# Windowed attention into a gated convolutional expert: stretches of 384 tokens with wide matmuls, gates on two chunks at once, and a different preparation of the first eight head pairs and of the weights

## The chip, the cores and the metric

The kernel runs on one core of a Trainium2 chip. A core has a tensor engine (PE, with a weight-load side PEld), a vector engine (DVE), a scalar engine (ACT), GpSimd (POOL) and SyncE (SP, which here issues the transfers). The metric is the device time of one execution in microseconds, the median of several runs. All times below are microseconds unless marked ns.

## The reference

```python
# q, k, v: (8, 8, 576, 64); batch 8, heads 8, sequence 576, head size 64
scores = q @ k^T / 8
# heads 0-3: 0 <= i - j < 32;  heads 4-7: 0 <= i - j < 128 and (i - j) % 4 == 0
scores = where(mask, scores, -1e9)
attn = exp(scores - max); attn = attn / (sum + 1e-9)
x = (attn @ v) laid out as (8, 576, 512)
h = relu(x @ w_in)                        # 512 -> 1024
conv = conv_w[0]*h[s-1] + conv_w[1]*h[s] + conv_w[2]*h[s+1]    # along the sequence, per channel
out = (h * sigmoid(conv)) @ w_out         # 1024 -> 512
```

Inputs and outputs are float32; the weights `w_in`, `w_out` and `conv_w` arrive as float64.

## The kernel before

**Attention.** It is computed for a batch and a pair of heads at a time (32 pairs: 8 batches times 4). Only 64 keys are scored for each block of 32 queries. On PE, `scores` (L248) issues 76 or 72 small matmuls into an `att` tile of PSUM. DVE then adds the mask (L254, L257), takes the maximum of each of the nine slots of 64 keys (L260) and subtracts it (L262). ACT takes the exponential of the whole 128x576 tile (L264). DVE sums it by slot (L266), adds 1e-9 (L268), inverts (L270), multiplies (L271) and transposes (L273). `values` (L283) issues 96 small matmuls. The result goes from PSUM to two float32r tiles, a high part `x..a` (ACT, L320) and the low rest `x..b`: subtracted by DVE (L335), or for the first two batches (`HELPED`) by PE with a negated identity (`minus`, L327 and L330) and copied by ACT (L333).

**Expert.** `expert(b)` works on a batch of 576 tokens. Every product of float32 operands is three float32r matmuls (high*high, high*low, low*high: `TERMS`). `first` (L353) multiplies by `w_in`: 8 chunks of 128 channels, each in two halves of 288 tokens, so 192 matmuls of 288 columns with the weights stationary. ACT applies relu (L360). The gate of each chunk of 576 tokens is ACT L371 (middle tap), twice DVE L365 (outer taps), ACT L376 (sigmoid), DVE L378 (times h), ACT L380 (high part `g..a`), DVE L382 (low part `g..b`). `second` (L395) multiplies by `w_out` with the weights stationary: 4 chunks of the output, 2 halves, 8 chunks of the sum, 3 terms, again 192 matmuls of 288 columns. ACT copies out of PSUM (L402), SP sends.

**Weights.** A float64 chunk of 128x512 is turned into a float32r high and low part by integer steps: ACT L428, DVE L430, L433, L435, L438, L441. For the first ten of the sixteen chunks (`SUMMED = 10`) PE adds the two words and forms the rest (L450, an fp32 matmul with the identity, L451 and L452 with `minus`; ACT L447 and L455 copy). For the other six DVE does it (L457, L463).

**What sets the order.** The program is written out as tasks with an engine, a cost, a due time, predecessors and buffers. `Planner.order` lists them for all engines once, when the program is built; a task that is ready and due first is taken. The due times are the tables `DUE`, `PAIR`, `WI`, `WO`, from the third batch on with a fixed period. Each engine works through its own list in order. Buffers are counted: two `qk`, three `v`, two `pt`, seven `x`, eight `g`, three `h`, three `c`, two PSUM banks each for `mm` and `nn`, and one `att` of four banks.

## Time and profile before

| | |
|---|---|
| median of 3 runs | 549.85 (548.9 to 550.44) |
| profiled execution, span first to last instruction | 549.1 |
| TensorE clock, mean granted | 0.990 |
| PE / PEld / DVE / ACT busy | 522.4 / 497.2 / 415.7 / 298.1 |
| instructions | 19084 |
| HBM read / written | 41.66 MB / 9.44 MB |

What lies around the span of the profiled execution is not listed for it; its span is 0.75 below the median of the timed runs. "Busy" is the time in which at least one instruction of the engine was under way; PE's matmuls are pipelined, so their own durations overlap (a 288-column matmul has 296 ns, and the next starts long before that). How long a matmul holds the engine is read from the chain of work that ended last, where a run of matmuls is one piece with its count.

### The profile page before, as it was taken

To read this page: it belongs to the slowest core of one execution; us is meant where nothing else is said; L and a number is where in the kernel's file an instruction comes from. 1 tells how busy PE (TensorE), PEld (TensorE's weight loads), DVE (VectorE), ACT (ScalarE), POOL (GpSimd) and SP (SyncE) were. 2 spreads that over 40 slices of the span, in tenths; PEclk is the share of its full clock that TensorE was granted. 3 is DMA by queue.
4 is the path that set the end of the run, shared out by engine and by line. 5 is a ranking of instruction groups with operands and counts; after the bars stand their busy time and mean duration, and the time that the engine had idled before them with its cause. 6 is when DMAs were issued, how large, how long until landed. Compare 5 with 4: busy or idle time off the path is not lost.

```text
span 549.1 us, 19084 instructions
## 1 busy us (share of the span) xinstructions
PE 522.4 (95%) x8664; PEld 497.2 (91%) x8664; DVE 415.7 (76%) x695; ACT 298.1 (54%) x556; POOL 0.9 (0%) x12
## 2 busy tenths in 40 slices
PE   3499978999999999999999999999999999999997
PEld 2468876999999999999999999999989999999997
DVE  4968998899997389946998389946988389946920
ACT  2457784855752486337742486237742486337721
POOL 0000000000000000000000000000000000000000
PEclk9999996999999999999999999999999999999999
DMA  7756513331044102630055102530045102300011
GB/s 247 268 157 215 195 52 137 119 121 44 7 138 152 30 23 65 200 110 23 13 161 170 32 23 72 190 113 23 17 152 162 45 23 58 117 26 23 0 44 44
DMA packets 17072, 52.31 MB, mean 95 GB/s; under 512 B 2016, under 2 KB 3168, under 8 KB 16992
## 3 DMA queue, kind: packets, MB, share of 16 engines
q1 hardware_dynamic: 16848, 51.02, 27.8%
q8 instruction: 68, 1.11, 0.9%
q10 hardware_dynamic: 144, 0.08, 0.1%
q14 instruction: 12, 0.10, 0.1%
HBM read 41.66 MB, written 9.44 MB: 93 GB/s over the span
## 4 chain that ended last, share of the span: by engine, by line
PE 92%; DVE 3%; ACT 2%; DMA 2%; issue 1%; ACTq 0%
PE nn L395 38%; PE mm L353 35%; PE att L283 8%; PE att L248 6%; PE nn L450 2%; PE nn L353 2%; PE att L327 1%; DMA qk<-in_qk_d_dram 1%; DMA qk<-in_qk_p_dram 1%; PE nn L451 0%; PE nn L452 0%; DVE pt L273 0%; DVE s L271 0%; PE att L330 0%; DVE c L365 0%
## 5 line engine op out<-in xcount | busy, mean ns | idle before, releaser
L365 DVE SCALAR_TENSOR_TENSOR c<-h,conv_sb,c 128x576 f32<-128x576 f32 x128 | 103.9, 815 | 48.4 <-ACT c L371 46.9
L360 ACT ACTIVATE h<-mm 128x288 f32<-128x288 f32 x120 | 48.8, 408 | 50.4 <-PE mm L353 50.1
L402 ACT COPY out<-nn 128x288 f32<-128x288 f32 x64 | 25.5, 400 | 70.1 <-PE nn L395 66.1
L378 DVE TENSOR_TENSOR c<-c,h 128x576 f32<-128x576 f32 x64 | 47.6, 755 | 9.4 <-ACT c L376 7.8
L283 PEld LDWEIGHTS att<-pt,v 32*64 32x64 f32 x3072 | 40.8, 138 | 14.8 <-DVE s L257 4.6
L283 PE MATMUL att<-pt,v 32*64 32x64 f32 (+2 forms) x3072 | 44.2, 232 | 9.4 <-DVE s L257 3.5
L371 ACT ACTIVATE c<-h,conv_sb 128x576 f32<-128x576 f32 x64 | 49.7, 776 | 1.3
L248 PE MATMUL att<-qk 64*32 64x64 f32 x2432 | 36.2, 235 | 11.0 <-DMA qk<-in_qk_d_dram 5.5
L248 PEld LDWEIGHTS att<-qk 64*32 64x32 f32 x2432 | 30.2, 111 | 16.9 <-DMA qk<-in_qk_d_dram 5.5
L376 ACT ACTIVATE c<-c 128x576 f32<-128x576 f32 x64 | 42.5, 678 | 2.1 <-DVE c L365 1.6
L353 PE MATMUL mm<-x2a,wi 128*128 128x288 f32 x144 | 40.5, 296 | 0.0
L353 PE MATMUL mm<-x1a,wi 128*128 128x288 f32 x144 | 40.3, 296 | 0.0
L353 PE MATMUL mm<-x3a,wi 128*128 128x288 f32 x144 | 40.3, 295 | 0.0
L353 PE MATMUL mm<-x0a,wi 128*128 128x288 f32 x144 | 40.3, 295 | 0.0
L395 PE MATMUL nn<-g2a,wo 128*128 128x288 f32 x128 | 37.0, 304 | 0.0
L395 PE MATMUL nn<-g0a,wo 128*128 128x288 f32 x128 | 36.4, 299 | 0.2
L395 PE MATMUL nn<-g6a,wo 128*128 128x288 f32 x128 | 36.6, 299 | 0.0
L395 PE MATMUL nn<-g3a,wo 128*128 128x288 f32 x128 | 36.4, 299 | 0.0
L395 PE MATMUL nn<-g1a,wo 128*128 128x288 f32 x128 | 36.4, 299 | 0.0
L395 PE MATMUL nn<-g4a,wo 128*128 128x288 f32 x128 | 36.4, 299 | 0.0
L395 PE MATMUL nn<-g5a,wo 128*128 128x288 f32 x128 | 36.4, 299 | 0.0
L395 PE MATMUL nn<-g7a,wo 128*128 128x288 f32 x128 | 36.1, 300 | 0.1
(194 smaller groups left out, 1502.5 us busy)
## 6 DMA issues: line engine op xcount, KB each, us to landing
...
```

The costliest lines, as they stand in the source:

```text
L248: nc.tensor.matmul(sc.t[quad * 32:quad * 32 + 32, slot // 4, slot % 4 * W:slot % 4 * W + W], q, k, start=i == 0, stop=i == len(parts) - 1, ...
L283: nc.tensor.matmul(tv.t[hd * 64:hd * 64 + 64, bank, o:o + n], v.t[quad * 32:quad * 32 + 32, block // 2, block % 2 * 64:block % 2 * 64 + 64 ...
L327: nc.tensor.matmul(tv.t[:, t, 0:128], minus, main[:, t], start=False, stop=True, skip_group_check=True)
L353: nc.tensor.matmul(ps.t[:, 0:HALF], wi[jw][fc][:, k * 128:k * 128 + 128], x[k].t[jx][:, hf * HALF:hf * HALF + HALF], start=(k == 0 and i = ...
L360: relu.append(plan.add("ACT", 0.4, due + 1.6 * u + 1.6, lambda fc=fc, hf=hf, ps=ps: nc.scalar.activation(out=h[fc].t[:, 1 + hf * HALF:1 + ...
L365: nc.vector.scalar_tensor_tensor(out=c[fc].t, in0=h[fc].t[:, k:S + k], scalar=conv_sb[:, k, fc:fc + 1], in1=c[fc].t, op0=ALU.mult, op1=ALU ...
L371: t = plan.add("ACT", 0.777, d, lambda fc=fc: nc.scalar.activation(out=c[fc].t, in_=h[fc].t[:, 1:S + 1], func=AF.Copy, scale=conv_sb[:, 1, ...
L376: t = plan.add("ACT", 0.686, d + 1.0, lambda fc=fc: nc.scalar.activation(out=c[fc].t, in_=c[fc].t, func=AF.Sigmoid), [t], [c[fc]], "sigmoid")
L378: t = plan.add("DVE", 0.755, d + 1.5, lambda fc=fc: nc.vector.tensor_tensor(out=c[fc].t, in0=c[fc].t, in1=h[fc].t[:, 1:S + 1], op=ALU.mult ...
L395: nc.tensor.matmul(ps.t[:, 0:HALF], wo[jw][2 * dm + k // 4][:, k % 4 * 128:k % 4 * 128 + 128], g[k].t[jg][:, hf * HALF:hf * HALF + HALF], ...
L402: outs.append(plan.add("ACT", 0.4, out_due + 3.3 + 3.3 * u, lambda hf=hf, ps=ps, o=o: nc.scalar.copy(out=o.t[:, hf * HALF:hf * HALF + HALF ...
L450: nc.tensor.matmul(ps.t, ident, t(), start=True, stop=False)
```

## The change

The expert works on stretches of 384 tokens, two segments of 192, three stretches to two batches (`expert(u)`, 12 stretches). `x` of two neighbouring batches lies in one wide tile per pair with a zero column between, and `first` (L410) computes both segments with a token more at each side: 388 columns. `second` (L452) turns the operands round: the gated tokens are stationary (128 of them), `w_out` streams with 512 columns, and the output has tokens on partitions. The gates handle the taps chunk by chunk (384 columns) and the sigmoid and the products two chunks at once (768 columns). There are five `g` tiles of two chunks and two `h` tiles of two chunks.

For the first eight pairs (`SLOTS`, `MASKS`, two batches) PE adds the mask by a bf16 identity before the scores (L269), DVE takes the negated maximum straight from PSUM (L288) and scales it (L295), and ACT takes the exponential in nine instructions, one for each slot, with the maximum as bias and the sum as a second output (L300). All sixteen weight chunks are summed by PE (`SUMMED = 16`). The due times are a new table without a period.

```diff
-HALF = S // 2
+UNITS = 3
+SEG, SEGS = S // 3, 2
+HALO = SEG + 2
+UNIT = SEGS * SEG
+XB = S + 1
+XW = 2 * XB + 2
+SLOTS, MASKS, HELPED = 0xff, 0xff, 0xff
+SUMMED = 16
+DUE = {
...
+    "pair": ((268.04, 269.22, 317.89, -93.12), (361.15, 413.68, 341.56, 430.48), ...
-    slots("x", 7, [128, S], F32R, 2)
-    slots("g", NF, [128, S], F32R, 2)
-    hs = slots("h", 3, [128, S + 2])
-    slots("c", 3, [128, S])
+    xt = [[const.tile([128, XW], F32R, name=f"x{p}{'ab'[j]}") for j in range(2)] for p in range(NP)]
...
+    slots("g", 5, [128, 2, UNIT], F32R, 2)
+    slots("h", 2, [128, 2 * SEGS, HALO])
+    slots("c", 3, [128, 2 * SEGS, SEG])
-    SUMMED = 10
-    HELPED = 2
+        def masks():
+            for i, n in enumerate((256, 256, W)):
+                nc.tensor.matmul(sc.t[:, i, 0:n], eye, mask_sb[:, kind, 256 * i:256 * i + n], start=True, stop=False,
+                                 skip_group_check=True)
+        if masked:
+            lq = plan.add("PE", 0.27, due, masks, [lq], [qk, sc, s], "E")
+            if masked:
+                for i, cost in enumerate((0.68, 0.215)):
+                    last = plan.add("DVE", cost, due + 2.0, lambda i=i: nc.vector.tensor_reduce(
+                        out=(m.t[:, 0:8].rearrange("p (h a) -> p h a", h=2), m.t[:, 8:9])[i],
+                        in_=(sc.t[:, 0:2, 0:256].rearrange("p h (a k) -> p h a k", k=W), sc.t[:, 2, 0:W])[i],
+                        axis=AX.X, op=ALU.max, negate=True), [last], [sc, s, m])
+            last = plan.add("DVE", 0.173, due + 2.5, lambda: nc.vector.tensor_scalar(
+                out=m.t, in0=m.t, scalar1=SCALE, scalar2=None, op0=ALU.mult), [last], [m])
+            def exps():
+                for i in range(9):
+                    nc.scalar.activation(out=s.t[:, i], func=AF.Exp,
+                                         in_=sc.t[:, i // 4, i % 4 * W:i % 4 * W + W] if masked else s.t[:, i], bias=m.t[:, i:i + 1],
+                                         scale=SCALE, accum_out=z.t[:, i:i + 1])
...
+            def first(fc, ps, k):
                 for i, (jw, jx) in enumerate(TERMS):
+                    nc.tensor.matmul(ps.t[:, 0:SEGS * HALO], wi[jw][fc][:, k * 128:k * 128 + 128], window(xt[k][jx]),
+                                     start=(k == 0 and i == 0), stop=(k == NC - 1 and i == 2))
...
+        for i in range(NF // 2):
+            d, convs = gated + 3.94 * i, []
+            for fc in (2 * i, 2 * i + 1):
+                t = plan.add("ACT", 0.617, ... AF.Copy, scale=conv_sb[:, 1, fc:fc + 1]), [relu[fc], conved], [h[i], c[i]])
+                for k in (0, 2):
+                    t = plan.add("DVE", 0.617, d + 0.5 + fc % 2, lambda fc=fc, k=k: tap(fc, k), [t], [h[i], c[i]])
+                convs.append(t)
+            t = plan.add("ACT", 0.846, ... AF.Sigmoid), convs, [c[i]], "sigmoid")
+            t = plan.add("DVE", 0.957, ... op=ALU.mult), [t], [c[i], h[i]])
+            hi = plan.add("ACT", 0.835, ... nc.scalar.copy(out=split(g[i].t[0]), in_=c[i].t), ...
+            gates.append(plan.add("DVE", 0.957, ... op=ALU.subtract), [hi], [c[i], g[i]]))
+        for j in range(UNIT // 128):
+            def second(j, ps, k):
                 for i, (jw, jg) in enumerate(TERMS):
+                    nc.tensor.matmul(ps.t, g[k // 2].t[jg][:, k % 2, j * 128:j * 128 + 128], wo[jw][k],
+                                     start=(k == 0 and i == 0), stop=(k == NF - 1 and i == 2))
+            for k in range(NF):
+                last = plan.add("PE", 0.648, out_due + 5.2 * j + 0.65 * k, lambda a=(j, ps, k): second(*a),
+                                [last, *(wored if u == 0 else []), gates[k // 2]], [ps, g[k // 2]], "E")
```

The order is settled when the program is built, so it can be shown for three places. In the rows a name is followed by its buffer's number; `g0a` and `g0b` are the high and low part of a gate tile, `wi_67` and `wo_84` are weight tiles.

PE, before, behind the first batch's `first` products: two weight chunks and a pair's rest, then the first matmuls of `second`, then the next pair's `values`.

```order
L450 MATMUL nn_163<-w0b,ident 128x512
L451 MATMUL nn_163<-r_157,minus 128x512
L452 MATMUL nn_163<-wo_82,minus 128x512
L327 MATMUL att_159<-x6a,minus 128x128 x4
L330 MATMUL att_159<-x6a,minus 128x32 x2
L450 MATMUL nn_162<-w1b,ident 128x512
L451 MATMUL nn_162<-r_158,minus 128x512
L452 MATMUL nn_162<-wo_83,minus 128x512
L395 MATMUL nn_163<-g0a,wo_82 128x288
L395 MATMUL nn_163<-g0b,wo_82 128x288
L395 MATMUL nn_163<-g0a,wo_90 128x288
L283 MATMUL att_159<-pt_113,v_101 64x64 x24
```

PE, after, at the corresponding place. The first `second` matmuls of the first stretch (L452) stand behind `first` matmuls (L410) of the second stretch.

```order
L410 MATMUL mm_148<-x3a,wi_68 128x388
L410 MATMUL mm_148<-x3b,wi_68 128x388
L410 MATMUL mm_148<-x3a,wi_76 128x388
L264 MATMUL att_147<-qk_100 32x64 x36
L452 MATMUL nn_151<-wo_83,g0a 128x512
L452 MATMUL nn_151<-wo_83,g0b 128x512
L452 MATMUL nn_151<-wo_91,g0a 128x512
L410 MATMUL mm_149<-x0a,wi_69 128x388
L410 MATMUL mm_149<-x0b,wi_69 128x388
L410 MATMUL mm_149<-x0a,wi_77 128x388
L410 MATMUL mm_149<-x1a,wi_69 128x388
L410 MATMUL mm_149<-x1b,wi_69 128x388
```

The ten PE-summed chunks stood ahead of the first `second` matmul, and now all sixteen do; between the first three matmuls of `second` and its next 21 PE now has four runs of twelve `first` matmuls and a pair's scores.

DVE, before, at the first gates of the first batch: a tile is one chunk of 576 tokens.

```order
L378 TENSOR_TENSOR c_147<-c_147,h_144 128x576
L378 TENSOR_TENSOR c_148<-c_148,h_145 128x576
L365 SCALAR_TENSOR_TENSOR c_149<-h_146,conv_sb,c_149 128x576
L382 TENSOR_TENSOR g0b<-c_147,g0a 128x576
L254 TENSOR_TENSOR s_103<-att_159,mask_sb 128x512
L382 TENSOR_TENSOR g1b<-c_148,g1a 128x576
L257 TENSOR_TENSOR s_103<-att_159,mask_sb 128x64
L378 TENSOR_TENSOR c_149<-c_149,h_146 128x576
L260 TENSOR_REDUCE m_106<-s_103 128x9
L262 TENSOR_TENSOR s_103<-s_103,m_106 128x576
L382 TENSOR_TENSOR g2b<-c_149,g2a 128x576
```

One instruction made one gate tile's step, and the maximum of a pair (L260) stood between. DVE, after, at the gates of the first stretch (`g0b` to `g3b` are what the 21 matmuls behind the rows above read): a tile is two chunks of 384.

```order
L439 TENSOR_TENSOR c_135<-c_135,h_133 128x768
L439 TENSOR_TENSOR c_136<-c_136,h_134 128x768
L443 TENSOR_TENSOR g0b<-c_135,g0a 128x768
L443 TENSOR_TENSOR g1b<-c_136,g1a 128x768
L306 TENSOR_REDUCE m_109<-s_106 128x9
L423 SCALAR_TENSOR_TENSOR c_137<-h_133,conv_sb,c_137 128x384 x2
L308 TENSOR_TENSOR s_106<-s_106,m_109 128x576
L423 SCALAR_TENSOR_TENSOR c_137<-h_133,conv_sb,c_137 128x384 x2
L423 SCALAR_TENSOR_TENSOR c_135<-h_134,conv_sb,c_135 128x384 x2
L439 TENSOR_TENSOR c_137<-c_137,h_133 128x768
L423 SCALAR_TENSOR_TENSOR c_135<-h_134,conv_sb,c_135 128x384 x2
L282 TENSOR_TENSOR s_104<-att_147,mask_sb 128x512
```

Each product and split now covers two chunks, and steps of a later batch's attention (L282, L306, L308) stand between the gates of the first stretch.

PE at the end of the program, before: the last `first` matmuls of the last batch, then the `second` matmuls of the same batch alone.

```order
L353 MATMUL mm_161<-x3a,wi_73 128x288
L353 MATMUL mm_161<-x3b,wi_73 128x288
L353 MATMUL mm_161<-x3a,wi_81 128x288
L353 MATMUL mm_161<-x0a,wi_73 128x288
L353 MATMUL mm_161<-x0b,wi_73 128x288
L353 MATMUL mm_161<-x0a,wi_81 128x288
L395 MATMUL nn_163<-g0a,wo_82 128x288
L395 MATMUL nn_163<-g0b,wo_82 128x288
L395 MATMUL nn_163<-g0a,wo_90 128x288
```

PE at the end of the program, after: the last `first` matmuls of the last stretch (into `mm_148`), then `second` of the stretch ahead of it (reading `g0`), whose 48 matmuls stand before the last stretch's 72.

```order
L410 MATMUL mm_148<-x2a,wi_74 128x388
L410 MATMUL mm_148<-x2b,wi_74 128x388
L410 MATMUL mm_148<-x2a,wi_82 128x388
L410 MATMUL mm_148<-x3a,wi_74 128x388
L410 MATMUL mm_148<-x3b,wi_74 128x388
L410 MATMUL mm_148<-x3a,wi_82 128x388
L452 MATMUL nn_151<-wo_83,g0a 128x512
L452 MATMUL nn_151<-wo_83,g0b 128x512
L452 MATMUL nn_151<-wo_91,g0a 128x512
L452 MATMUL nn_151<-wo_84,g0a 128x512
L452 MATMUL nn_151<-wo_84,g0b 128x512
L452 MATMUL nn_151<-wo_92,g0a 128x512
```

The last batch's own products stood directly behind its gates; now another stretch's products lie between.

More of the change, by code (lines that the diff above doesn't have):

```diff
@@ L167, in attn_moe @@
     minus = const.tile([128, 128], F32R, name="minus")
+    eye = const.tile([128, 128], BF16, name="eye")
     wi = [[const.tile([128, 512], F32R, name=f"wi{j}{c}") for c in range(NF)] for j in range(2)]
-    wo = [[const.tile([128, 512], F32R, name=f"wo{j}{c}") for c in range(2 * NC)] for j in range(2)]
+    wo = [[const.tile([128, DM], F32R, name=f"wo{j}{c}") for c in range(NF)] for j in range(2)]
     plan = Planner()
@@ L260, in attention @@
-        last = plan.add("DVE", 0.755, due + 2.0, lambda: nc.vector.tensor_reduce(
-            out=m.t, in_=s.t, axis=AX.X, op=ALU.max), [last], [s, m])
-        last = plan.add("DVE", 0.755, due + 2.5, lambda: nc.vector.tensor_tensor(
-            out=s.t, in0=s.t, in1=wide(m.t), op=ALU.subtract), [last], [s, m])
-        last = plan.add("ACT", 0.685, due + 3.0, lambda: nc.scalar.activation(
-            out=s.t, in_=s.t, func=AF.Exp, scale=SCALE), [last], [s], "exp")
-        last = plan.add("DVE", 0.755, due + 3.5, lambda: nc.vector.tensor_reduce(
-            out=z.t, in_=s.t, axis=AX.X, op=ALU.add), [last], [s, z])
+        two = lambda t: (halves(t[:, 0:512]), t[:, 512:576])
@@ L332, in attention @@
             last = plan.add("PE", (0.42, 0.6)[kind], due + 7.2, less, his, [tv, x], "E")
             return [plan.add("ACT", cost, due + 7.5, lambda i=i: nc.scalar.copy(out=parts(x.t[1])[i], in_=src(i)),
-                             [last], [tv, x]) for i, cost in ((0, (0.62, 1.12)[kind]), (1, (0.25, 0.3)[kind]))]
-        return [plan.add("DVE", cost, due + 7.5, lambda i=i: nc.vector.tensor_tensor(
+                             [last], [tv, x]) for i, cost in pieces]
+        return [plan.add("DVE", cost + 0.06 * (1 - i), due + 7.5, lambda i=i: nc.vector.tensor_tensor(
@@ L346, in expert @@
         relu = []
-        for u in range(2 * NF):
-            fc, hf = u // 2, u % 2
-            ps, last = Buffer("nn" if b == 0 and u % 4 > 1 else "mm"), None
-            def first(fc, hf, ps, k):
+        for fc in range(NF):
+            ps, last = Buffer("nn" if u == 0 and fc % 2 else "mm"), None
+            def first(fc, ps, k):
                 for i, (jw, jx) in enumerate(TERMS):
-                    nc.tensor.matmul(ps.t[:, 0:HALF], wi[jw][fc][:, k * 128:k * 128 + 128],
-                                     x[k].t[jx][:, hf * HALF:hf * HALF + HALF],
+                    nc.tensor.matmul(ps.t[:, 0:SEGS * HALO], wi[jw][fc][:, k * 128:k * 128 + 128], window(xt[k][jx]),
@@ L355, in first @@
                                      start=(k == 0 and i == 0), stop=(k == NC - 1 and i == 2))
             for k in range(NC):
-                last = plan.add("PE", 0.396, due + 1.6 * u + 0.4 * k, lambda a=(fc, hf, ps, k): first(*a),
-                                [last, wired[fc], *(ready[k] if b == 0 else sum(ready, []))], [ps, x[k]], "E")
-            relu.append(plan.add("ACT", 0.4, due + 1.6 * u + 1.6, lambda fc=fc, hf=hf, ps=ps: nc.scalar.activation(
-                out=h[fc].t[:, 1 + hf * HALF:1 + hf * HALF + HALF], in_=ps.t[:, 0:HALF], func=AF.Relu),
-                [last], [ps, h[fc]]))
+                last = plan.add("PE", 0.493, first_due + 1.97 * fc + 0.49 * k, lambda a=(fc, ps, k): first(*a),
+                                [last, wired[fc], *(t for b in used for t in (ready[b][k] if u == 0 else sum(ready[b], [])))],
+                                [ps, *x[k]], "E")
@@ L364, in tap @@
+            relu.append(plan.add("ACT", 0.49, first_due + 1.97 * fc + 1.97, lambda fc=fc, ps=ps: nc.scalar.activation(
+                out=both(h[fc // 2].t, fc).rearrange("p a k -> p (a k)"), in_=ps.t[:, 0:SEGS * HALO], func=AF.Relu),
+                [last], [ps, h[fc // 2]]))
         def tap(fc, k):
-            nc.vector.scalar_tensor_tensor(out=c[fc].t, in0=h[fc].t[:, k:S + k], scalar=conv_sb[:, k, fc:fc + 1],
-                                           in1=c[fc].t, op0=ALU.mult, op1=ALU.add)
+            t = both(c[fc // 2].t, fc)
@@ L368, in expert @@
+            nc.vector.scalar_tensor_tensor(out=t, in0=both(h[fc // 2].t, fc)[:, :, k:k + SEG], in1=t,
+                                           scalar=conv_sb[:, k, fc:fc + 1], op0=ALU.mult, op1=ALU.add)
+        split = lambda t: t.rearrange("p f (a k) -> p (f a) k", a=SEGS)
         gates = []
[L369 to L384 removed]
```

177 lines of the change are left out of this document (96 added, 81 removed).

## The prediction

> **What bounds the kernel now.** I read the page's busy times first, then the chain that ended last, then that chain in order of time, then a table by stretches, and last the groups by line.
>
> ```profile
> span 549.1 us, 19084 instructions
> PE 522.4 (95%) x8664; PEld 497.2 (91%) x8664; DVE 415.7 (76%) x695; ACT 298.1 (54%) x556; POOL 0.9 (0%) x12
> ...
> PE 92%; DVE 3%; ACT 2%; DMA 2%; issue 1%; ACTq 0%
> ```
>
> The first line is the span. The second gives busy time, share and instructions of each engine. The last gives the shares of the chain that ended last: PE carries 92% of it. The span of this execution stands 0.75 below the median of 549.85; the sum is made against 549.1, and 0.75 is added at the end.
>
> ```profile
> 0.00:94.60 94.60, 72.76 (x1556) 61.03 (x1557) 80.54 (x157) 54.47 (x103) 0.90 (x12) 0.95 0.53 184
> ...
> 140.00:518.70 378.70, 378.00 (x6429) 365.89 (x6428) 289.45 (x464) 207.34 (x387) 0.00 (x0) 1.00 0.24 79
> 518.70:526.20 7.50, 6.94 (x48) 6.19 (x46) 5.48 (x8) 4.20 (x8) 0.00 (x0) 1.00 0.01 2
> ```
>
> Each row is a stretch, its length, then busy time (and instructions) of PE, PEld, DVE, ACT, POOL, then clock and transfers. From 140 to 518.7 PE is busy 378.0 of 378.7, DVE 289.5 (76%), ACT 55%. So the middle is PE's alone. In the first 94.6, when the first `second` matmul starts, PE is busy 72.8, while DVE is busy 80.5 (85%): the head waits on DVE.
>
> ```profile
> 305.80 7.94 PE mm L353 x60
> 316.54 16.30 PE mm L353 x123
> 367.45 7.94 PE mm L353 x60
> ```
>
> A row of this chain is a start, how long that piece held the path, and its instructions. The same piece of 60 matmuls starts at 305.80 and at 367.45: a batch takes 61.65. One matmul of 288 columns holds PE 16.30/123 = 0.1325, so its 384 take 50.9, and the other 10.8 are four pairs' scores and values, 2.69 each with the changes between matmul shapes.
>
> ```profile
> 53.08 0.86 PE nn L450 x2
> 53.94 0.23 PE nn L451
> 54.18 0.23 PE nn L452
> ...
> 58.18 0.39 PE att L327 x4
> 58.57 0.18 PE att L330 x2
> ...
> 81.98 1.27 PE att L283 x76
> ...
> 90.35 0.43 PE nn L451
> 90.78 0.43 PE nn L452
> ```
>
> In the head, a weight chunk takes 0.86 + 0.23 + 0.23 = 1.32 and a pair's rest by PE 0.39 + 0.18 = 0.57. PE's own work is therefore 8 × 61.65 + 10 × 1.32 + 8 × 0.57 = 511.0, and 38.1 of the span is something else. PE's last run ends at 545.6 (the tail rows below), which leaves 3.5 behind it; in 518.7 to 526.2, where the last gates are finished, PE does 48 matmuls (6.4) in 7.5, a loss of 1.1; 33.5 are left for the head. There, between 74.26 and 81.98, the path leaves PE altogether, and afterwards the same L451 and L452 take 0.43 instead of 0.23, at the clock of 0.50 of this row:
>
> ```profile
> 84.00:93.00 9.00, 8.18 (x113) 6.42 (x114) 8.79 (x17) 4.09 (x8) 0.00 (x0) 0.50 0.54 183
> ```
>
> ```profile
> 526.24 19.36 PE nn L395 x144
> 545.66 0.40 ACT out L402
> ```
>
> **The wide matmuls.** `first` has 12 × 8 × 4 × 3 = 1152 matmuls of 388 columns for 1536 of 288; `second` has 12 × 3 × 8 × 3 = 864 of 512 for 1536. Columns are 889,344 against 884,736, so all that can be gained is what a matmul costs beside its columns. No 388 is in the trace, but 512 is: L452 (128x512, float32r, another weight load behind it) holds the path 0.23. From 288 to 512 that is 0.0975 for 224 columns, so 388 takes 0.176. Sum: 1152 × 0.176 + 864 × 0.230 = 401.5 against 3072 × 0.1325 = 407.0: 5.5 less. Lower bound: at the clock of 0.50 L451 and L452 take 0.43; if all of that scaled with the clock, 512 would take 0.215 and 388 0.163, together 373.6, 33.4 less than now. Upper bound: if cost follows columns at the 288 rate, 0.1785 and 0.2356, together 409.2, 2.2 more. I take 0.230, since it is measured at full clock in the same form. The weight load does not explain the 288 row: the L327 row loads four full weights in 0.39, 0.1 each.
>
> The Trainium skill (TensorE: Matmul & The Clock Gate, section "Wait — 56ns, not 53.3ns?") gives a warm matmul as columns/2.4 plus about 2.5 ns. By it 512 would take 0.2158, 388 0.1642 and 288 0.1225; this trace has 0.23 and 0.1325, so it disagrees on both that can be compared.
>
> **More for PE.** Six more chunks summed by PE: 6 × 1.32 = 7.9, on the path. Masks: three bf16 matmuls for each of eight pairs, 576 columns; between nothing and the 0.39 of L327's four, near the latter: 0.3 × 8 = 2.4. The rest by PE stays 8 × 0.57. PE's work becomes 511.0 − 5.5 + 7.9 + 2.4 = 515.8.
>
> **DVE.**
>
> ```profile
> L365 DVE SCALAR_TENSOR_TENSOR c<-h,conv_sb,c 128x576 f32<-128x576 f32 x128 | 103.9, 815 | 48.4 <-ACT c L371 46.9
> L378 DVE TENSOR_TENSOR c<-c,h 128x576 f32<-128x576 f32 x64 | 47.6, 755 | 9.4 <-ACT c L376 7.8
> L254 DVE TENSOR_TENSOR s<-att,mask_sb 128x512 f32<-128x512 f32 x32 | 21.8, 680 | 2.4 <-PE att L248 2.3
> L257 DVE TENSOR_TENSOR s<-att,mask_sb 128x64 f32<-128x64 f32 x32 | 6.6, 208 | 0.0
> L262 DVE TENSOR_TENSOR s<-s,m 128x576 f32<-128x576 f32 x32 | 24.1, 753 | 0.7
> L266 DVE TENSOR_REDUCE z<-s 128x9 f32<-128x576 f32 x32 | 23.7, 739 | 0.4 <-ACT s L264 0.3
> L268 DVE TENSOR_SCALAR z<-z 128x9 f32<-128x9 f32 x32 | 5.4, 170 | 0.9
> L270 DVE RECIPROCAL z<-z 128x9 f32<-128x9 f32 x32 | 6.9, 215 | 1.0
> L271 DVE TENSOR_TENSOR s<-s,z 128x576 f32<-128x576 f32 x32 | 24.2, 758 | 1.0
> L273 DVE STREAM_TRANSPOSE pt<-s 128x576 f32<-128x576 f32 x32 | 24.8, 776 | 0.9
> L435 DVE SCALAR_TENSOR_TENSOR w1b<-out,w1b 128x512 int32<-128x512 int32 x8 | 5.5, 686 | 0.1
> L438 DVE TENSOR_SCALAR w0a<-w0b 128x512 int32<-128x512 int32 x8 | 3.4, 422 | 0.1
> L463 DVE TENSOR_TENSOR wo<-w1b,wo 128x512 fp32r<-128x512 f32 x3 | 2.1, 688 | 0.0
> ```
>
> Behind the first bar stand busy us and mean ns. 512 against 64 elements (L254, L257) is 1.05 ns an element, so a tap of 384 takes 0.815 − 0.20 = 0.613, a step of 768 0.755 + 0.20 = 0.957. Gates of all batches: 192 × 0.613 + 96 × 0.957 = 209.6 against 128 × (0.815 + 0.755) = 201.0: +8.6, hidden in the middle, where DVE has 24% free; if that cover goes, see the rivals. In each of the eight first pairs the mask adds (0.888), the subtraction (0.753) and the sum (0.739) go, the scale (0.170) comes, and the maximum is read from PSUM in two pieces (0.888 for about 0.74): 2.06 less, 16.5 in all. Six chunks lose two steps of 0.688: 8.3 less. Both fall in the head.
>
> **The head.** The 21 `second` matmuls of the first stretch wait for `g3b`. Ahead of it the new order has on DVE: 16 chunks of 3 × 0.422 + 2 × 0.686 = 2.64 (42.2); eight pairs of 0.680 + 0.208 + 2 × 0.170 + 0.215 + 0.758 + 0.776 = 2.98 (23.8); four steps each of two later pairs (4.8); 16 taps (9.8); eight steps of 768 (7.7); about 3 for masks and conv weights: 91.3. Neighbours overlap a little: means times counts over all DVE rows make 442 where the page has 415.7 busy, so 91.3 is 85.8 busy. At the 85% of the head before, `g3b` is done at 101. PE's work ahead of that place is 168 × 0.176 + 3 × 0.230 + 16 × 1.32 + 8 × 0.57 + 8 × 0.3 + 11 scores and 8 values (9.5 × 2.69) = 83.8. Transfers are not in the way: the same 16 chunks and eight pairs come on SP, in another order, and the output is the same bytes in 36 transfers for 36. GpSimd zeroes more columns beside the first transfer.
>
> ```profile
> L264 ACT ACTIVATE s<-s 128x576 f32<-128x576 f32 x32 | 21.3, 684 | 21.8 <-DVE s L262 21.7
> L455 ACT CAST wi<-nn 128x512 fp32r<-128x512 f32 x8 | 4.7, 584 | 6.1 <-PE nn L452 6.0
> L333 ACT CAST x1b<-att 128x64 fp32r<-128x64 f32 x2 | 0.6, 284 | 0.0
> L360 ACT ACTIVATE h<-mm 128x288 f32<-128x288 f32 x120 | 48.8, 408 | 50.4 <-PE mm L353 50.1
> ```
>
> ACT has 54.5 busy in the first 94.6. Nine exponentials of 64 replace one of 576: from 512 to 64 elements (L455, L333) is 0.3 less, so 0.684 shrinks to about 0.3 each, the second output unseen. It could be free (0.27) or double it (0.6); I take 0.3, since L333's 0.284 is the nearest row. That is 8 × (2.7 − 0.684) = 16.1, and six more copies of 0.584, 3.5: 74 of 101, under DVE's 86. In the middle ACT is 45% free, and its instructions there get fewer and wider (relu 96 × 0.49 for 128 × 0.408). Behind the nine stand on ACT the copies of weight chunks (L499, L507), for which PE's sums wait.
>
> There is one `att` tile, and scores and values of all pairs take turns in it. Before, the scores left it with the mask add; now the nine exponentials read it.
>
> ```profile
> 0.74 4.69 DMA qk<-in_qk_d_dram
> ...
> 342.39 1.06 PE att L248 x66
> 363.18 1.29 PE att L283 x81
> ```
>
> A pair holds it for 0.3 + 1.06 + 0.888 + 0.170 + 2.7 = 5.1 from the mask to the last exponential, and for 1.29 + 0.87 + 0.57 + 0.87 = 3.6 from the values to the last copy: 8.7. Eight pairs make 69.6, three later pairs' scores and mask adds 5.8, and the first transfer lands at 5.4: 81 with no wait between the steps. Each pair changes engine eight times, and behind engines this busy each change may wait half of an instruction of 0.6: 8 × 8 × 0.3 = 19, together 100. Two bounds, 101 and 100, that hinder each other: I take 103. The head then loses 103 − 83.8 = 19 where it lost 33.5. What is late next is this tile, ahead of DVE: scores that wait for it hold every matmul behind them on PE.
>
> **The end.** The last gates now run beside the preceding stretch's 48 matmuls, 48 × 0.23 = 11.0, longer than a chain of about 0.49 + 0.62 + 2 × 0.61 + 0.84 + 0.96 + 0.83 + 0.96 = 5.9 (ACT steps by 0.8 ns an element from their rows); the 1.1 goes. The last copy is 0.584 for 0.40 and its transfer nearly doubles: 3.5 becomes 4.0.
>
> Sum: 515.8 + 19 + 4.0 = 538.8, plus 0.75: 539.6, so 540.
>
> **Rivals.** *Wide matmuls shed their fixed cost* (lower bound, 0.163 and 0.215): 27.9 less, 512. For it: the low-clock rows show no fixed part. Against: L452 shows 0.23 every time at full clock. The Trainium skill's formula, above, would come out beside it (1.4 and 0.7 more in sum, about 514); the trace has so far not followed it. *Cost follows columns*: 7.7 more, 547. For it: 0.1325/288 and 0.23/512 differ by 2.4%. *The `att` tile bounds the head*, the case on the other side: if an exponential with its sum takes 0.6 instead of 0.3, every pair holds the tile 2.7 longer, 8 × 2.7 = 21.6, the 21 matmuls start at about 122 and the head loses 38: 515.8 + 38 + 4.75 = 559. It decides from a head of 115 (a loss of 31), that is from about 0.47 an exponential. For it: no row shows an exponential of 64 or a second output. Against it: a copy of 64 from PSUM takes 0.284 (L333). *The middle waits on the gates*: five `g` tiles of two chunks and two `h` tiles let gates lead by little; DVE's 50 of 60 us a batch would have to leave PE idle 3% to give back all: 550. Against it: DVE then still has a sixth free. *No gain in the head*, where the change does not do what it says there, gives 515.8 + 33.5 + 4.75 = 554.
>
> **Chances.** Forecast (532 to 546) 0.50; shed cost (506 to 524) 0.24; by columns (546 to 549) 0.05; waits in the middle (547 to 556) 0.08; the `att` tile or no gain in the head (548 to 562) 0.13. The range leaves out the ends of the outer cases, about 0.2 in all: 509 to 552. The three runs of before lie within 0.3%, about what tells a change from none. Faster by more than that (under 548.2): 0.50 + 0.24 + 0.04 + 0.03 = 0.81; within it (to 551.5): 0.06; slower: 0.13.
>
> **What would show it.** Chain pieces of `first` at 0.176 a matmul and `second` at 0.230 (0.163 and 0.215 for the first rival, 0.236 for the second); the first 21-matmul run of `second` at about 103; L300 at about 300 ns; PE over 98% busy from 120 to the end; nothing but a copy and a transfer behind the last matmul. The prediction is wrong if the head is late because the exponentials hold `att`, if PE's rows wait for `g` in the middle, or if the wide rows are far from 0.176 and 0.230.

## The result, and the profile after

The changed kernel takes 557.59 (median of 4 runs, 556.71 to 558.69) against 549.92 of the kernel before on the same chip: ratio 1.0137, interval 1.0112 to 1.0162. It is slower; the forecast was 540.

The page of its profiled execution (556.71; span, busy times, the chain's shares):

```profile
span 554.9 us, 17158 instructions
PE 528.1 (95%) x7656; PEld 456.8 (82%) x7656; DVE 401.7 (72%) x700; ACT 328.1 (59%) x652; POOL 1.5 (0%) x30
...
PE 92%; ACT 5%; DVE 1%; DMA 1%; issue 0%; ACTq 0%; DVEq 0%
```

The chain in order of time, after: the last runs ahead of the 21 `second` matmuls of the first stretch (24 with the three behind them), long runs of `second` and `first` in the middle, and the end.

```profile
109.66 8.56 PE mm L410 x48
118.22 0.90 PE att L264 x58
119.12 5.67 PE nn L452 x24
...
149.66 16.37 PE nn L452 x72
...
225.60 17.08 PE mm L410 x96
...
524.02 27.24 PE nn L452 x120
```

A matmul of 388 columns holds PE 17.08/96 = 0.178, one of 512 16.37/72 = 0.227; behind the last one 3.6 are left. The 21 matmuls start at 119.12, and not because they wait for the gates: DVE's step for `g3b` (L443) starts at 113.76 and takes 0.95, so it is done at 114.7, while PE still has 4.4 of earlier work to do. Stretches, after (columns as in the prediction):

```profile
0.00:62.00 62.00, 39.69 (x847) 27.08 (x847) 42.31 (x97) 35.45 (x135) 1.50 (x30) 0.81 0.65 221
0.00:94.60 94.60, 72.29 (x1486) 54.09 (x1487) 68.26 (x151) 61.02 (x221) 1.50 (x30) 0.87 0.59 200
140.00:518.70 378.70, 378.67 (x5264) 336.26 (x5264) 278.38 (x463) 219.11 (x348) 0.00 (x0) 1.00 0.22 73
```

The same first 62 us of the kernel before:

```profile
0.00:62.00 62.00, 44.71 (x1086) 37.44 (x1087) 48.94 (x104) 31.79 (x61) 0.90 (x12) 1.00 0.60 206
```

The middle has no gap: PE is busy 378.67 of 378.70. So the loss is in the head, 554.9 − 515.8 − 3.6 = 35.5 (33.5 before, 19 forecast). DVE, which was to set the head at 85%, is busy 68.26 of the first 94.6 (72%). At 62.7 the steady work of `first` begins, and from there to 119.12 PE is busy 55.67 of 56.42. By 62.7 it has done 9 weight sums, 5 masks, 4 pairs' values and rests, scores of 5 and 7 matmuls of `first`, by the rows of the prediction 29.0 of work. So 33.7 of the 35.5 are lost by that moment; the kernel before had done 40.1 by then. What PE waited for, and a pair and a half on the chain, after:

```profile
PE att L329 <- ACT s L300: 7.9, 3, 3.9
...
PE att L269 <- ACT s L300: 3.4, 2, 2.0
```

```profile
29.30 0.64 PE att L269 x3
29.94 1.28 PE att L264 x68
31.22 0.02 issue
31.25 0.83 DVE m L288 x2
32.08 0.02 issue
32.10 0.18 DVE m L295
32.33 0.04 issue
32.37 2.78 ACT s L300 x18
35.15 0.04 issue
35.20 1.87 PE att L329 x81
37.07 2.00 PE nn L502 x2
39.07 0.26 PE nn L503
39.33 0.25 PE nn L504
39.60 0.59 ACT wo L507
40.19 0.70 ACT x0b L382 x2
40.89 0.04 issue
40.93 1.26 PE att L329 x76
```

Shares of the chain from 24.6 to 62.7, by line:

```profile
by line: ACT s L300 22.0%; PE nn L502 21.4%; PE att L329 13.6%; PE att L264 9.7%; DVE m L288 4.4%; PE nn L504 4.2%; PE nn L503 4.1%; PE att L374 3.9%; PE att L269 3.8%; ACT x3b L382 1.9%; PE att L377 1.9%; ACT x1b L382 1.8%; ACT x0b L382 1.
```

The first of these lists gives total, times and longest. Both its rows are waits for the one `att` tile: the values (L329) that start at 35.20 belong to the pair before, whose transposed exponentials were done at 27.3, and they wait until the nine exponentials of the next pair have read the tile. The second list is one engine after another with no slack between: mask, scores, maximum, nine exponentials (18 instructions), the values of the pair before, a weight sum, copies, the next values. Such a chain says where the path ran, not what a piece is worth if it is shortened; the experiments say that.

### The profile page after: what moved, and what is told of

Its sections match the earlier page's. It is cut to its first block, busy times and chain, and to the rows that moved or that the text cites. A ratio compares the mean times of both kernels' runs of the same rounds, so it can differ in the third digit from the quotient of the medians.

```text
span 554.9 us, 17158 instructions
## 1 busy us (share of the span) xinstructions
PE 528.1 (95%) x7656; PEld 456.8 (82%) x7656; DVE 401.7 (72%) x700; ACT 328.1 (59%) x652; POOL 1.5 (0%) x30
## 4 chain that ended last, share of the span: by engine, by line
PE 92%; ACT 5%; DVE 1%; DMA 1%; issue 0%; ACTq 0%; DVEq 0%
PE nn L452 37%; PE mm L410 36%; PE att L329 7%; PE att L264 6%; ACT s L300 3%; PE nn L502 3%; PE nn L410 1%; DMA kinds_sb<-in_mask_dram 1%; DVE m L288 1%; PE att L269 1%; PE att L374 1%; PE nn L504 1%; PE nn L503 1%; ACT wo L507 0%; ACT c L437 0%
## 5 line engine op out<-in xcount | busy, mean ns | idle before, releaser
L423 DVE SCALAR_TENSOR_TENSOR c<-h,conv_sb,c 128x384 f32<-128x384 f32 x192 | 116.3, 616 | 31.7 <-ACT c L431 28.2
L417 ACT ACTIVATE h<-mm 128x388 f32<-128x388 f32 x92 | 45.0, 495 | 69.8 <-PE mm L410 61.8
L410 PE MATMUL mm<-x0a,wi 128*128 128x388 f32 x184 | 63.6, 346 | 0.0
L410 PE MATMUL mm<-x2a,wi 128*128 128x388 f32 x184 | 63.4, 344 | 0.0
L410 PE MATMUL mm<-x3a,wi 128*128 128x388 f32 x184 | 63.1, 343 | 0.0
L410 PE MATMUL mm<-x1a,wi 128*128 128x388 f32 x184 | 62.5, 340 | 0.0
L431 ACT ACTIVATE c<-h,conv_sb 128x384 f32<-128x384 f32 x96 | 58.5, 617 | 3.9 <-DVE g2b L443 1.0
L329 PEld LDWEIGHTS att<-pt,v 32*64 32x64 f32 x3072 | 40.7, 138 | 19.9 <-ACT s L300 9.5
L439 DVE TENSOR_TENSOR c<-c,h 128x768 f32<-128x768 f32 x48 | 45.1, 952 | 11.7 <-ACT c L437 11.1
L329 PE MATMUL att<-pt,v 32*64 32x64 f32 (+2 forms) x3072 | 44.2, 232 | 8.9 <-ACT s L300 7.9
L452 PE MATMUL nn<-wo,g0a 128*128 128x512 f32 x120 | 43.9, 398 | 0.0
L452 PE MATMUL nn<-wo,g2a 128*128 128x512 f32 x120 | 43.9, 397 | 0.0
L452 PE MATMUL nn<-wo,g1a 128*128 128x512 f32 x120 | 42.9, 392 | 0.0
L452 PE MATMUL nn<-wo,g3a 128*128 128x512 f32 x108 | 39.8, 400 | 0.0
L452 PE MATMUL nn<-wo,g4a 128*128 128x512 f32 x108 | 39.4, 397 | 0.0
L410 PEld LDWEIGHTS mm<-x0a,wi 128*128 128x128 f32 x184 | 34.7, 189 | 1.8 <-ACT h L417 0.3
L410 PEld LDWEIGHTS mm<-x2a,wi 128*128 128x128 f32 x184 | 34.7, 189 | 0.8
L282 DVE TENSOR_TENSOR s<-att,mask_sb 128x512 f32<-128x512 f32 (+1 forms) x48 | 20.4, 449 | 20.2 <-PE att L264 20.1
```

The costliest lines, as they stand in the source:

```text
L282: last = plan.add("DVE", cost, due + 1.5, lambda i=i: nc.vector.tensor_tensor(out=two(flat())[i], in0=scored()[i], in1=two(mask_sb[:, kind ...
L329: nc.tensor.matmul(tv.t[hd * 64:hd * 64 + 64, bank, o:o + n], v.t[quad * 32:quad * 32 + 32, block // 2, block % 2 * 64:block % 2 * 64 + 64 ...
L410: nc.tensor.matmul(ps.t[:, 0:SEGS * HALO], wi[jw][fc][:, k * 128:k * 128 + 128], window(xt[k][jx]), start=(k == 0 and i == 0), stop=(k == ...
L417: relu.append(plan.add("ACT", 0.49, first_due + 1.97 * fc + 1.97, lambda fc=fc, ps=ps: nc.scalar.activation(out=both(h[fc // 2].t, fc).rea ...
L423: nc.vector.scalar_tensor_tensor(out=t, in0=both(h[fc // 2].t, fc)[:, :, k:k + SEG], in1=t, scalar=conv_sb[:, k, fc:fc + 1], op0=ALU.mult, ...
L431: t = plan.add("ACT", 0.617, d + fc % 2, lambda i=i, fc=fc: nc.scalar.activation(out=both(c[i].t, fc), in_=both(h[i].t, fc)[:, :, 1:SEG + ...
```

## Experiments

Runs of 3 rounds each, beside the kernel before (549.6 to 550.6 in the five groups). The first ten change what a task issues and keep the changed kernel's order, so that the order cannot be the reason.

**1. The tile set free.**

```diff
+            return   # masks() issues nothing
-                    ... nc.vector.tensor_reduce(out=..., in_=sc.t[...], axis=AX.X, op=ALU.max, negate=True)
+                    ... nc.vector.tensor_tensor(out=two(flat())[i], in0=scored()[i], in1=two(mask_sb[:, kind])[i], op=ALU.add)
+                nc.vector.tensor_reduce(out=m.t, in_=s.t, axis=AX.X, op=ALU.max, negate=True)
-                    ... in_=sc.t[:, i // 4, ...], bias=m.t[:, i:i + 1], ...
+                    ... in_=s.t[:, i], bias=m.t[:, i:i + 1], ...
```

> Same order of tasks as the changed kernel, but DVE adds the mask while it moves the scores out of PSUM, as in the kernel before (two instructions of 0.69 and 0.22 in place of the two maxima), takes the maximum from SBUF (0.755 more per pair), and the nine exponentials read SBUF. So the one att tile is given back after the add, 3.5 us earlier per pair (9.1 to 12.7 becomes free, 13.0 to 15.7 no longer holds it), and DVE has 8 x 0.755 = 6.0 us more. Theory A (the att tile, held from the mask through the nine exponentials, makes the head a serial chain): the wait between the exponentials and the next pair goes, 8 pairs x 2.7 us less 0.75 each, so 8 to 14 us less: 544 to 550. Theory B (PE's sixteen weight sums in its in-order queue set the head): within 3 of the changed kernel's 557.6. Theory C (the low TensorE clock in the gaps): within 3, as the gaps become other gaps. Theory D (DVE is the bound, as the prediction took it): 4 to 6 us more, 562 to 564.

555.05, ratio 1.0088 (1.0056 to 1.0120): 2.5 less, with DVE's 6.0 more in it; not the 8 to 14 of theory A. The nine now read SBUF and hold the chain longer, and PE, whose waits for the exponentials to leave the tile are gone, waits for ScalarE's copies of weight chunks, which stand behind the nine:

```profile
11.62 3.10 ACT s L302 x18
```

```profile
PE nn L504 <- ACT wi L509: 6.2, 3, 3.3
```

**2. Short exponentials.**

```diff
-                for i in range(9):
-                    nc.scalar.activation(out=s.t[:, i], ..., bias=m.t[:, i:i + 1], accum_out=z.t[:, i:i + 1])
+                nc.scalar.activation(out=halves(flat()[:, 0:512]), in_=sc.t[:, 0:2, 0:256], func=AF.Exp, scale=SCALE)
+                nc.scalar.activation(out=flat()[:, 512:576], in_=sc.t[:, 2, 0:W], func=AF.Exp, scale=SCALE)
+                nc.scalar.activation(out=z.t, in_=m.t, func=AF.Exp, scale=SCALE)
```

> Same order of tasks as the changed kernel; in place of nine exponentials with a bias and a sum each (2.7 to 2.8 us a pair) ScalarE does one of 512 columns, one of 64 (both straight from PSUM, some 0.9 together) and a small one of 9 columns that stands for the sums. Maximum and slot sums are left out of the result. The att tile is held as before, from the mask on, but some 1.5 us shorter per pair. Theory A: 8 x 1.5 = 12 us less, 545 to 548. Theory B or C: 3 us less at most, 554 to 557.6. Theory D (DVE the bound): no change, 556 to 559.

544.43, ratio 0.9894 (0.9859 to 0.9930): 13.2 less. The nine, by their groups after; the short ones; and the first 62 us with these:

```profile
L300 ACT ACTIVATE s<-att,m 128x64 f32<-128x64 f32 x72 | 21.5, 327 | 8.1 <-DVE m L295 6.6 <-PE nn L504 1.5
L300 ACT ACTIVATION_READ_ACCUMULATOR s<-att,m 128x1 f32 x72 | 15.8, 220 | 0.0
```

```profile
L299 ACT ACTIVATE s<-att 128x512 f32<-128x512 f32 x8 | 4.8, 596 | 7.8 <-DVE m L288 7.8
L300 ACT ACTIVATE s<-att 128x64 f32<-128x64 f32 x8 | 1.8, 220 | 0.0
L301 ACT ACTIVATE z<-m 128x9 f32<-128x9 f32 x8 | 1.7, 215 | 0.0
```

```profile
0.00:62.00 62.00, 46.80 (x1054) 32.69 (x1055) 48.02 (x110) 33.25 (x77) 1.50 (x30) 0.92 0.72 250
```

ScalarE's busy time over the span fell by 15.2 (328.1 to 312.9), DVE's work stayed, and PE did 7.1 more in the first 62. The same 24 `second` matmuls start at 107.95. Theory D falls, and B and C with their 3 at most; theory A's 545 to 548 is the nearest. This kernel leaves the maximum and the sums out of its result, so it is an experiment and not a version to use; run 6 likewise.

**3. The clock.**

```diff
+            if (b, p) in FILLED:   # (0, 3), (0, 0), (0, 1), (0, 2), (1, 2), (1, 0)
+                for _ in range(8): nc.tensor.matmul(mms[1][0], eye, mask_sb[:, 0, 0:512], **ONE)
```

> Same order of tasks as the changed kernel, with eight more matmuls of 512 bf16 columns (a product nobody reads, in a PSUM bank not yet in use) behind the scores of six of the first eight pairs, 1.8 us at full clock each time, where PE otherwise waits for maxima and exponentials. Theory C (some 24 us at half clock in the first 63, from PE's gaps, cost the head): the clock stays full and the work that stood at half, some 10 us of PE, comes 6 to 8 us earlier: 549 to 552. Theory A: the clock may rise but the chain through maxima and exponentials stays: 3 us less at most, 554 to 558. Theory B (PE's queue in the chain): the fill delays it: 2 to 6 us more.

556.32, ratio 1.0109 (1.0077 to 1.0140): 1.3 less, about what the runs can tell. The clock of this stretch of the changed kernel had been 0.57 (0.91 here), and the core's mean with the idle matmuls was nearly full (0.978 before them):

```profile
20.00:40.00 20.00, 15.57 (x291) 10.83 (x291) 14.40 (x31) 12.04 (x50) 0.00 (x0) 0.57 0.46 161
```

```profile
core 0: 553.6 us, clock 0.997
```

The mean clock was mended and the time hardly: theory C's 549 to 552 falls. But the idle matmuls have a price: two of their six groups stand on the chain with 1.83 each (at 16.87 and 66.11), and the steady work of `first` begins at 58.89 in place of 62.71. What a full clock without them would bring is not shown.

**4. Six chunks back on DVE.**

```diff
+                if not by_pe:   # by_pe is false for chunks 2 to 7 of w_out
+                    nc.vector.tensor_tensor(out=lo, in0=t(), in1=hi.bitcast(F32), op=ALU.subtract); return
                 nc.tensor.matmul(ps.t, ident, t(), start=True, stop=False)
```

> Same order of tasks as the changed kernel; for six weight chunks (the last six of w_out, four of which stand in the first 50 us) the remainder is added and the low part taken by DVE, as in the kernel before, in place of TensorE's sums: PE has 6 x 1.32 = 7.9 us less at full clock, 6 x 2.4 at half, DVE 6 x (0.69 + 0.56) = 7.5 more. Theory B (sixteen sums in PE's in-order queue set the head): 8 to 10 us less, 547 to 550. Theory A (the att tile's chain): only the sums that stand between one pair's values and the rest of it shorten the chain, three or so by 2 us, and PE has less to do behind it: 3 to 7 less, 551 to 555. Theory D (DVE the bound of the head): 0 to 7 us more.

561.57, ratio 1.0207 (1.0169 to 1.0244): 4.0 more, though L502 to L504 were 30% of the chain above. Theory B falls. The result lies where theory D put it, 0 to 7 more: DVE's 7.5 more count here, and PE's two waits for the exponentials grew from 7.9 and 3.4 to 9.4 and 10.1.

**5. The softmax of before.**

```diff
...   # mask added by DVE as in run 1
+                nc.vector.tensor_reduce(out=m.t, in_=s.t, axis=AX.X, op=ALU.max)
+                nc.vector.tensor_tensor(out=s.t, in0=s.t, in1=wide(m.t), op=ALU.subtract)
+                nc.scalar.activation(out=s.t, in_=s.t, func=AF.Exp, scale=SCALE)   # for the nine
+            nc.vector.tensor_reduce(out=z.t, in_=s.t, axis=AX.X, op=ALU.add)
```

> Same order of tasks as the changed kernel, but the first eight pairs do their softmax as the kernel before did the later ones: DVE adds the mask, takes the maximum, subtracts it and sums the slots, and ScalarE does one exponential of 576 columns. Per pair DVE has 0.90 + 3 x 0.755 = 3.17 in place of 1.06 us (8 x 2.1 = 17 more), ScalarE 0.68 in place of 2.78 (17 less), and att is given back after the add. Theory E (DVE and ScalarE wait for each other in turn along each pair's softmax, so that what DVE was relieved of came back as ScalarE's time on the same chain: 0.89 + 0.17 + 2.78 = 3.84 now, 3.85 here): 553 to 561. Theory A (holding the att tile through the exponentials is what costs): 545 to 550. Theory D (DVE's sum of work is the bound): 567 to 575.

561.27, ratio 1.0198 (1.0181 to 1.0216): 3.7 more, just above theory E's 553 to 561. Moving that work from DVE to ScalarE gains at this order, though far from the 17 of DVE's time. ScalarE waits here at the head of its list for DVE, which it did for 6.6 after:

```profile
ACT s L301 <- DVE s L296: 24.2, 8, 5.0
```

**6. Time put back on ScalarE.**

```diff
+                for i in range(7):   # behind the short exponentials of run 2
+                    nc.scalar.activation(out=idle, in_=mask_sb[:, 0, 64 * i:64 * i + 64], func=AF.Exp, ..., accum_out=idle_sum[:, i:i + 1])
```

> The kernel with the short exponentials (544.4) with ScalarE's time given back to it off the chain: behind the two exponentials and the small one stand seven exponentials of 64 columns on a scratch tile, some 2.1 us per pair, which nothing waits for. Maximum and slot sums are left out of the result as there. Theory E (the length of the chain through the exponentials counts, ScalarE has room): 544 to 548. Theory F (ScalarE's queue is full in the head, and any 17 us put on it cost it): 554 to 558.

555.83, ratio 1.0092 (1.0065 to 1.0118): 11.4 above run 2. The time put back:

```profile
L305 ACT ACTIVATE idle<-mask_sb,ident 128x64 f32<-128x64 bf16 x56 | 19.5, 348 | 1.6
L305 ACT ACTIVATION_READ_ACCUMULATOR idle<-mask_sb,ident 128x1 f32 x56 | 10.6, 189 | 0.0
```

Nobody reads these instructions, and the pair's own three exponentials are as short as in run 2; they only stand in ScalarE's list. Nearly all that run 2 gained is gone, as theory F said. But with their second records they are more than what run 2 took away: ScalarE is busy 21.9 more than in run 2 (334.8 for 312.9) and 6.7 more than in the changed kernel, which is still 1.8 slower. So the list counts for most, and the shorter stay on the chain and on the tile for something: at 11.4 for 21.9, the 15.2 of run 2 are 8 of its 13.2 (an estimate that takes the price as even).

**7. One maximum for each row.**

```diff
+                        out=m.t[:, i:i + 1], in_=scored()[i], axis=(AX.XY, AX.X)[i], op=ALU.max, negate=True)
+                for i in range(2):
+                    nc.scalar.activation(out=two(flat())[i], in_=scored()[i], func=AF.Exp, bias=m.t[:, 2:3], scale=SCALE)
```

> Same order of tasks as the changed kernel, mask by TensorE, but one maximum for each row of the tile (over all nine slots) in place of one for each slot, so that two exponentials with one bias (512 and 64 columns, 0.9 us) do the work of nine (2.78); the slot sums go to DVE, one instruction of 0.755 per pair more. Theory E (the chain's length): 8 x (1.9 - 0.755) = 9 us less, 546 to 550. Theory A (how long att is held): 8 x 1.9 = 15 less at most, 542 to 546. Theory D (DVE the bound): 6 us more, 562 to 565.

554.52, ratio 1.0072 (1.0053 to 1.0092): 3.1 less, short of every theory that expected a gain and better than theory D. What ScalarE waited for:

```profile
ACT s L299 <- DVE m L294: 10.0, 7, 3.5
```

**8. Softmax and six sums undone.** Runs 4 and 5 together.

> Same order of tasks as the changed kernel, stretches of 384 tokens and wide matmuls kept, but the softmax of the first eight pairs and the last six weight chunks of w_out done as in the kernel before (the two undoings that cost 3.7 and 4.0 us by themselves, together). What is left of the change is then the stretches and the order. Theory G (the order costs most: it spreads the first four pairs over the first 53 us, with five chunks of w_out between them, where the kernel before had them done in 31 us): 563 to 567, that is 19 to 23 us above the 544 that the kernel before would take with the 5.5 us of the wide matmuls off. Theory H (each of the two edits costs, and they hide each other's cost): 550 to 558.

570.25, ratio 1.0374 (1.0353 to 1.0395). More than the two costs together (565.3), above both theories, and 26 above 549.6 − 5.5: with the work of the kernel before, the new stretches and order are much the slower ones. Together the two edits are worth 12.7 at this order.

**9. DVE loaded where it waits.**

```diff
+                for _ in range(2):   # behind the factor of the maxima
+                    nc.vector.tensor_reduce(out=idle_sum[:, 0:4], in_=ident.unsqueeze(1).to_broadcast([128, 4, 128]), axis=AX.X, op=ALU.max)
```

> The changed kernel with two more DVE instructions per pair of the first eight (a maximum over 512 numbers of a constant each, 0.68 us each, 10.9 together, which nobody reads), right behind the factor of the maxima, where the profile shows DVE waiting for the nine exponentials in six of eight pairs. Theory F with DVE to spare (ScalarE's queue is what is full, DVE waits for it): 556 to 560. Theory D (DVE the bound): 566 to 569. Theory E (both queues count): 560 to 565.

559.84, ratio 1.0185 (1.0151 to 1.0218): 2.3 more for 10.9 of work, at the border between theories F and E. DVE had room there; with run 6 this is the contrast: 21.9 more on ScalarE cost 11.4, about half, and 10.9 on DVE 2.3, about a fifth.

**10. No maximum.**

```diff
-                    last = plan.add("DVE", cost, due + 2.0, lambda i=i: nc.vector.tensor_reduce(..., op=ALU.max, negate=True), ...)
+                    last = plan.add("DVE", cost, due + 2.0, lambda: None, [last], [sc, s, m])
+                for i in range(2):
+                    nc.scalar.activation(out=two(flat())[i], in_=scored()[i], func=AF.Exp, scale=SCALE)
```

> Same order of tasks as the changed kernel; the first eight pairs take no maximum at all (the exponential of small scores needs none): two exponentials straight from PSUM in place of nine, slot sums by DVE. Per pair ScalarE has 1.9 us less, DVE 1.06 less and 0.755 more. Theory F (ScalarE's queue; 13.2 us came of 15 taken off it in the short exponentials, where DVE's work was as before): 541 to 546. Theory E with the slot sum's 0.755 on the chain at full: 546 to 550. In e7_row DVE had 6.0 us more and the time went up by 10 from the short exponentials; if those 10 are DVE's price, this one is at 545 less the price of 2.4: 541.

546.63, ratio 0.9943 (0.9924 to 0.9962): 11 less than the changed kernel, just above theory F's 541 to 546, and 0.6% faster than the kernel before. It holds for inputs whose scores the exponential can take without a maximum. Against run 7 DVE is relieved of 8 × 1.06 = 8.5, and 7.9 came of it; it was for just these maxima that ScalarE waited 10.0 there.

**11 to 14. Other orders.** Costs and due numbers of the planner are others; the stretches stay. In run 11 the work is that of run 8, in 12 the changed kernel's, in 13 and 14 that of runs 7 and 10 as tasks of their own.

```diff
-                last = plan.add("PE", 0.493, first_due + ...
+                last = plan.add("PE", 0.534, first_due + ...
-    "wi": (599.05, 423.59, 482.60, 375.93, 799.08, 653.39, 513.48, 522.88),
+    "wi": (-155.12, -204.84, -324.6, -231.83, -52.24, -57.88, -41.08, -30.19),
```

> The work of e8_both_undone (stretches of 384, wide matmuls, softmax and ten sums as in the kernel before; 570.3 us) in another order: other due numbers for pairs, chunks and stretches, and the planner's costs of six first and three second matmuls set to the 0.534 and 0.682 that the trace shows. Theory G (the order costs): 548 to 558. Theory S (the stretches cost, whatever the order): 564 to 572.

> The changed kernel's own work (557.6) in another order: other due numbers, and the planner's costs of the matmuls and of the nine exponentials set to what the trace shows (0.534, 0.682, 2.8). Most of the chunks come sooner, and the pairs stand as far apart as before, since each still holds att from the mask through nine exponentials. Theory G: 545 to 551. Theory F (ScalarE's nine exponentials set the head under any order): 554 to 560.

> The softmax of e7_row (one maximum for each row, two exponentials; 554.5 at the changed kernel's order) as tasks of their own, planned with their own costs and other due numbers: two pairs by 16 us of the plan, four by 33, and then the chunks. Theory G: 542 to 548. Theory F alone: 552 to 556.

> The softmax of e10_nomax (no maximum, two exponentials; 546.6 at the changed kernel's order) as tasks of their own, planned with their own costs and other due numbers, and with the first products of the first stretch in the two mm banks alone. Theory G: 537 to 543. Theory F alone: 545 to 549.

563.90 (1.0256, 1.0223 to 1.0289), 559.56 (1.0173, 1.0139 to 1.0208), 558.57 (1.0152, 1.0123 to 1.0181) and 548.05 (0.9973, 0.9955 to 0.9991). Run 11 gains 6.3 of the 26, just short of theory S; the others are 2.0, 4.1 and 1.4 slower than the same work in the changed kernel's order, runs 12 and 14 as theory F said, run 13 above both theories. In run 13 the fourth pair was transposed at 39.4 and not at 47.8 as in run 7, and yet by 80 us PE had been busy 56 in place of 63. Theory G, that the pairs' order is what costs, is not borne out; only the orders tried are excluded.

**15 to 17. Single parts put into the kernel before**, with its stretches and due numbers; the planner orders the tasks anew.

```diff
+        if masked:   # b < HELPED; runs 15 and 16
+            lq = plan.add("PE", 0.27, due, masks, [lq], [qk, sc, s], "E")
+            last = plan.add("ACT", 2.7, due + 3.0, exps, ...)          # run 15; run 16: two exponentials, 0.9
-    SUMMED = 10
+    SUMMED = 13                                                       # run 17
```

> The kernel before with one part of the change alone: in the first eight pairs TensorE adds the mask, ScalarE takes nine exponentials from PSUM; stretches, sums and due numbers as before, the order planned anew with them. Theory K (the edit helps wherever it stands, 3.7 us at the changed kernel's order): 541 to 547. Theory L (the edit holds the att tile 6 us longer per pair, and so breaks up the four pairs that the kernel before had done by 31 us; the new order is made round that): 555 to 566.

> The kernel before with the short softmax of e10_nomax in the first eight pairs (mask by TensorE, no maximum, two exponentials, slot sums by DVE), stretches, sums and due numbers as before. DVE has 8 x (0.90 + 2 x 0.755) = 19 us less in the head, ScalarE 8 x 0.2 more, att is held from the mask to the end of the exponentials, about as long as it was to the end of the add. Theory K: 19 us of DVE are worth 3 to 10 where DVE is the fullest engine of the head: 540 to 547. Theory L without its cause (att is not held longer here): 545 to 550.

> The kernel before with 13 chunks summed by TensorE in place of 10, nothing else: PE 3 x 1.32 = 4.0 more, DVE 3 x 1.25 = 3.7 less, half of the change's six. If PE's own work counts and nothing comes back: 553 to 555. If DVE's relief is worth what it was at the changed kernel's order (4.0 us for six): 547 to 549.

569.52 (1.0344, 1.0316 to 1.0372), 557.16 (1.0121, 1.0092 to 1.0150) and 553.22 (1.0057, 1.0036 to 1.0077). The softmax part alone, in the order that the planner makes for it, makes the kernel before 18.9 slower: theory L, and worse than it said. A shorter one that relieves DVE of 19 us still makes it 6.5 slower, outside both theories; the tile is not held longer there, so theory L's cause is not the whole. Run 15, its first 62 us, its middle, and two waits:

```profile
0.00:62.00 62.00, 39.11 (x891) 30.81 (x892) 32.55 (x79) 35.70 (x134) 0.90 (x12) 0.94 0.58 196
...
160.00:540.00 380.00, 379.73 (x6384) 368.15 (x6383) 289.35 (x463) 210.62 (x390) 0.00 (x0) 1.00 0.24 77
```

```profile
ACT s L285 <- DVE m L280: 15.0, 4, 7.8
...
PE att L254 <- ACT s L285: 9.9, 3, 4.0
```

PE is busy 5.6 less in the first 62 than in the kernel before and without a gap in the middle; DVE is busy 32.6 there where it was 48.9. Three more sums cost 2.6 of the 4.0 that PE does more.

**18. Run 10 with the idle matmuls of run 3.**

> The two edits that helped at the changed kernel's order together: the softmax without a maximum (546.6) and the eight idle matmuls behind the scores of six pairs (1.3 less there, as the clock stayed full). If they add: 544 to 546. If the shorter chain has closed the gaps that the idle matmuls fill (granted clock 0.994 as it is): 546 to 549.

550.56, ratio 1.0001 (0.9984 to 1.0018): 3.9 above run 10 (3.2 by the ratios), outside what was expected. They do not add: four of the six groups of idle matmuls now stand on the chain, 1.67 each (at 14.03, 26.22, 44.78 and 59.68).

## Why the prediction was wrong

- **Wide matmuls: right.** 0.178 and 0.227 for 0.176 and 0.230; 401.4 in sum for 401.5. "Shed cost" and "by columns" fall.
- **PE's other work: right.** From 119.12 to the end of PE's last run it takes 432.1, where the sum leaves 515.8 − 83.8 = 432.0.
- **The middle and the end: right.** PE is busy without a break beside gates that grew by 8.6 of DVE, the 1.1 before the last gates went, and the tail is 3.6 for 4.0.
- **The price of an exponential: right.** 2.78 for nine, 2.7 assumed. The rival that gave 559 was nearest in time (557.59), but by luck: its price, 0.6 each, did not come. What it said of the tile is borne out in part: PE waited for it (7.9 and 3.4), but setting it free gained 2.5 (run 1).
- **The head: the step that failed.** "Two bounds, 101 and 100, that hinder each other: I take 103." It was 119.1, a loss of 35.5 for 19. The tile's 100 was near: the last of the eight pairs' rests by PE ends at 103.3. DVE's 101 for `g3b` became 114.7 with DVE less busy than assumed, and even that was not what came last. Two things were wrong. First, sums of busy time were compared at the place of `g3b`, as if PE could do its 83.8 at any time before. It could not: until four pairs were through, at 62.7, only 29.0 of it could be had, and 62.7 + 83.8 − 29.0 is 117.5. Second, ScalarE was left out because 74 busy of 101 lay under DVE's 86. What counted was its list in order: the nine exponentials of 2.78 wait for DVE's maximum, keep the tile meanwhile from the values of the pair before, and stand ahead of the copies that PE's sums wait for (run 1). The prediction named what is queued there and gave it no price. Runs 2 and 6 are that price: 15.2 of ScalarE's time less brings 13.2, 21.9 put back takes 11.4; how the 13.2 divide between list, tile and chain is only estimated above. Without that time the changed kernel would be at 544.4, 4.8 from the forecast.
- **DVE's relief: not worth what was claimed.** 24.8 us less work was to shorten a head bound by DVE; DVE fell to 72% of the first 94.6. At the new order the two edits are worth 12.7 together (run 8); in the kernel before the softmax part alone cost 18.9 (run 15), three sums 2.6 (run 17).
- **Around the span** 0.75 was added; the median lies 2.7 above the span shown.

So 557.59 is 18.0 above 539.6: 16.5 from the head, 1.9 from around the span, 0.4 less from the tail. Still open is how the 26 of run 8 divide between stretches and order: run 11 recovered 6.3 by order, and stretches of 576 with the new order were not tried. Run 10 is the fastest version with a whole result, for inputs that need no maximum.
